# Two pages' first layers interwoven, the decoding of the dense weights reordered, and 512-column products in the dense layer

## The chip, the cores and the metric

The kernel runs on one core of one Trainium2 chip. The metric is the device time of one execution in microseconds (us). Engines are named as in the profile: PE (TensorE, matmuls; PEld its weight loads), DVE (VectorE), ACT (ScalarE), POOL (GpSimd) and SP (SyncE, which here only issues transfers). Each engine works off its own instructions in the order of the program; waits between engines are on semaphores.

## The reference

```python
def reference(x, expert_emb, tau, w1, w2, w_in, w_out):
    X = np.fft.fft(np.fft.fft(x, axis=1), axis=2).real        # x: 8 x 3072 x 256
    x = X.reshape(24576, 256)
    # routing: cosine of each token with 8 expert vectors, one expert a token
    xn = x / (norm(x) + 1e-6); en = expert_emb / (norm(expert_emb) + 1e-6)
    logits = xn @ en.T / tau
    e = argmax(logits, axis=1); gate_w = softmax(logits)[arange, e]
    y = gate_w[:, None] * (maximum(x @ w1[e], 0) @ w2[e])     # 256 -> 1024 -> 256
    # dense layer for every token
    h = y @ w_in                                              # 256 -> 2048
    return maximum(0.01 * h, h) @ w_out                       # 2048 -> 256
```

All is float32. `w_in` and `w_out` come as 64-bit floats, which the kernel takes apart itself.

## The kernel before

**Batches.** The two FFTs of a batch of 3072 tokens (`batch`) are matmuls with tables of sines and cosines between folds on DVE: folds (label `f`, L399 to L315), the stage along the sequence (`s_stage`, label `s`), then column tiles (`unit`, label `d`: two matmuls of L446, ACT's `cs`, DVE's `xo`), which also give the routing logits. `route` (label `r`) finds each token's expert and place, `pages` the list of pages; then POOL scatters 24 lists into the DRAM tables (label `sc`, L599). Batch 0 runs ahead of everything; batches 1 to 7 run as generators, a few labels in each step of the main loop, with a budget per step: each label has a weight (`WEIGHT`), and what is left of `WORK` is spread evenly over the steps up to a limit. `MARGIN` and `NEAR` set that limit for batch 1.

**Pages.** Tokens of one expert are gathered in pages of 256. There are 89 full pages, 21 half slots for what is left over, and seven pages made of those: 96 that go through the dense layer. `load_page` (SP) reads a page's entries of the three tables, `fetch_page` merges them on DVE (`merge`, L874 to L880) and gathers the rows with POOL; `transpose` turns them on PE into `xt`. `wload` (SP) loads a quarter of an expert's weights into one of two `raw` buffers, `wsplit` splits it in two parts (ACT L919 the high one, DVE L920 the rest).

**Steps.** A product of two float32 numbers is made of three fp32r products: high x high, high x low, low x high (`PASS`). The main loop goes over a list `steps` of (kind, page, s). Kind 1 is the expert layer in four steps: `m1_a` makes 256 columns of h (L941, twelve matmuls), `m1_b` adds them to `y` (L959). Kind 2 is the dense layer in eight steps: `m2_a` (L1014) and `m2_b`, which adds to `o` (L1045). Kind 3 is a half slot: its first layer (L973) has 512 columns to a matmul. Each step issues its a-part, then the b-part of a step `LAG` = 3 earlier (2 in the first steps). ACT and DVE make `hh` from `h` in between. After a page's eighth `m2_b`, ACT scales the two halves of `o` (L1051) and POOL scatters them to the output. PSUM has eight banks: two `a`, three `h`, two `o`, one `y`.

**Decoding.** `decodes` takes `w_in` and `w_out` apart in 16 pieces; `decode` is one piece of seven DVE instructions (L740 to L754) and three ACT copies. Before, two pieces run side by side, instruction by instruction, and the next two load when both are done. Six pieces (`NDEC`) run within batch 0, at a pace of steps per label (`RAMP`); the others within the first steps of the pages, seven instructions in a step (`DREST`).

Of the kernel before, what the change touches and what calls it, by code (L numbers as in the profile page):

```python
# [6 lines left out]
F32 = mybir.dt.float32  # L7
# [51 lines left out]
class K:  # L59
# [314 lines left out]
    def batch(self, b):  # L374
# [51 lines left out]
        if b:  # L426
            yield "f"
            yield "f"
        z = [mp.tile([128, 1537], F32, tag=f"z{j}", name="z") for j in range(2)]
# [87 lines left out]
    def route(self, b, rt, lr, n2, sli, tb, i0, i1):  # L517
# [54 lines left out]
        if b:  # L572
            yield "r"
            yield "r"
        pr = self.pa()[:, 0:E * (nt + 1)].rearrange("p (i e) -> p i e", e=E)
# [154 lines left out]
    def decode(self, raw, hi, lo, temps):  # L730
# [7 lines left out]
        nc.scalar.activation(b, lw.bitcast(U32), AF.Copy, scale=2.0 ** -52)  # L738
# [11 lines left out]
        V.tensor_tensor(b, b, t.bitcast(F32), op=ALU.mult)  # L750
# [5 lines left out]
    def decodes(self):  # L756
# [12 lines left out]
        raws = {}  # L769
        self.ndec = 0  # L770

        def load(i, tile):
            raws[i] = tile
            nc.sync.dma_start(out=tile if pieces[i][1] is None else tile.rearrange("p (c d) -> p c d", c=2), in_=pieces[i][0])

        def unit(i, temps):
            return self.decode(raws.pop(i).rearrange("p (f w) -> p f w", w=2), *pieces[i][2:], temps)


        def buf(i):  # L780
            if i < 2:
                return self.xp.tile([128, 1024], F32, tag="raw", name="rawd", bufs=2).bitcast(I32)
            return self.ip.tile([128, 1024], I32, tag="rawd", name="rawd", bufs=2)

        def temps():
            return [self.ip.tile([128, 512], F32, tag=f"dec{i}", name="dec", bufs=2) for i in range(3)]

        for i in range(4):
            load(i, buf(i))
        yield  # L790
        for i in range(0, NDEC, 2):
            pair = [unit(i + k, temps) for k in range(2)]
            while pair:
                for g in list(pair):
                    if next(g, "end") == "end":
                        pair.remove(g)
                        self.ndec += 1
                    else:
                        yield
            for k in range(2):  # L800
                if i + 4 + k < NDEC:
                    load(i + 4 + k, buf(2))
            yield
# [528 lines left out]
```

## Time and profile before

| | |
|---|---|
| Median of three runs | 3684.71 us (3683.41 to 3685.48) |
| The profiled execution | 3683.92 us, span 3682.2 us |
| PE busy | 3532.7 us, 96% of the span, 29441 matmuls |
| PE weight loads busy | 3501.5 us, 95% |
| DVE busy | 2334.4 us, 63% |
| ACT busy | 1933.6 us, 53% |
| POOL busy | 672.2 us, 18% |
| Mean granted clock of PE | 0.982 of 2.4 GHz |

Busy shares are means over the whole span. PE is busy 0.4 of the first two of 40 slices (92 us each) and 0.8 or more of every later one, so the first 200 us are read apart from the rest.

### The profile page before, as it was taken

Reading aid. Unit: us, or ns where it says so; the run is one execution under the profiler, and the core shown is the slowest. Engines: PE = TensorE matmul, PEld = TensorE weight load, DVE = VectorE, ACT = ScalarE, POOL = GpSimd, SP = SyncE. Lnnn points to the kernel's source line nnn. Section 1 sums busy time; section 2 is a strip of 40 time slices with the busy share of each in tenths; the row PEclk is TensorE's granted clock in tenths of the full one; section 3 lists DMA queues with packets and bytes.
Section 4 is the critical chain, followed back from the end, with each engine's and each line's share of the span. In section 5 each row is a group of like instructions: output and inputs, shape, how many; then the busy total and the mean of one; then the engine's idle time right before and its main releaser. Section 6 shows DMA issues by size and latency. Waiting matters only on the chain.

```text
span 3682.2 us, 74898 instructions
## 1 busy us (share of the span) xinstructions
PE 3532.7 (96%) x29441; PEld 3501.5 (95%) x29441; DVE 2334.4 (63%) x4595; ACT 1933.6 (53%) x3491; POOL 672.2 (18%) x620
## 2 busy tenths in 40 slices
PE   4498999999999999999999999999999999999998
PEld 3388999999999999999999999999999999999998
DVE  7575666567565666657565675657666566666644
ACT  3345446455554546445464455544565456666543
POOL 3113111311013110321114111231114111111100
PEclk8699999999999999999999999999999999999999
DMA  4332413233232322233132322223232245555300
GB/s 141 126 109 71 145 60 115 66 113 96 73 107 71 134 82 99 74 102 104 60 120 73 120 76 86 94 81 124 76 105 76 72 132 155 153 152 155 104 25 16
DMA packets 266165, 362.58 MB, mean 98 GB/s; under 512 B 75984, under 2 KB 216659, under 8 KB 265620
## 3 DMA queue, kind: packets, MB, share of 16 engines
q1 hardware_dynamic: 238896, 303.66, 25.9%
q0 software_dynamic: 25184, 52.35, 4.5%
q8 instruction: 230, 3.77, 0.4%
q10 hardware_dynamic: 1732, 1.79, 0.1%
q14 instruction: 123, 1.01, 0.1%
HBM read 304.64 MB, written 63.41 MB: 100 GB/s over the span
## 4 chain that ended last, share of the span: by engine, by line
PE 86%; issue 3%; DMA 1%; DVE 0%; ACT 0%; POOLq 0%; SPq 0%; POOL 0%; ACTq 0%
PE o L1045 27%; PE h L1014 26%; PE h L941 13%; PE y L959 13%; PE y L986 2%; PE h L973 2%; PE a L926 1%; PE a L446 1%; DMA out<-ob,tab 1%; PE a L1030 0%; PE a L339 0%; PE a L340 0%; PE a L337 0%; DMA raw<-w 0%; PE a L334 0%
## 5 line engine op out<-in xcount | busy, mean ns | idle before, releaser
L1045 PE MATMUL o<-wo,hh 128*128 128x256 f32 x9216 | 1233.9, 283 | 9.4 <-DVE hh L1034 9.4
L1014 PE MATMUL h<-yt,wi 128*128 128x256 f32 x9216 | 1217.1, 281 | 14.4 <-ACT yt L963 14.2
L1045 PEld LDWEIGHTS o<-wo,hh 128*128 128x128 f32 x9216 | 1148.5, 189 | 13.4 <-DVE hh L1034 10.0
L1014 PEld LDWEIGHTS h<-yt,wi 128*128 128x128 f32 x9216 | 1137.9, 189 | 14.8 <-ACT yt L963 14.4
L1016 ACT ACTIVATE g<-h 128x512 f32<-128x512 f32 x768 | 457.6, 596 | 788.0 <-PE h L1014 786.7
L1017 DVE TENSOR_TENSOR g<-g,h 128x512 f32<-128x512 f32 x768 | 525.9, 685 | 459.9 <-ACT g L1016 456.3
L1052 POOL DMA_INDIRECT out<-ob,tab x192 | 214.8, 1119 | 2298.7 <-ACT ob L1051 1932.4
L920 DVE TENSOR_TENSOR w<-raw,w 128x1024 fp32r<-128x1024 f32 x440 | 536.9, 1224 | 151.7 <-ACT w L919 148.6
L944 DVE SCALAR_TENSOR_TENSOR hh<-h,hh 128x512 fp32r<-128x512 f32 x356 | 246.2, 691 | 548.8 <-ACT hh L943 548.7
L941 PE MATMUL h<-xt,w 128*128 128x256 f32 x4272 | 563.4, 281 | 17.1 <-ACT xt L928 14.8
L959 PE MATMUL y<-hh,w 128*128 128x256 f32 x4272 | 567.6, 282 | 8.4 <-ACT w L919 7.1
L941 PEld LDWEIGHTS h<-xt,w 128*128 128x128 f32 x4272 | 530.4, 190 | 18.8 <-ACT xt L928 15.7
L959 PEld LDWEIGHTS y<-hh,w 128*128 128x128 f32 x4272 | 529.8, 189 | 9.9 <-ACT w L919 7.5
L1034 DVE TENSOR_TENSOR hh<-g,hh 128x512 fp32r<-128x512 f32 x768 | 525.9, 685 | 1.4 <-ACT hh L1033 1.3
L919 ACT ACTIVATE w<-raw 128x1024 fp32r<-128x1024 f32 x440 | 462.1, 1055 | 89.1 <-DMA raw<-w 86.7
L1033 ACT ACTIVATE hh<-g 128x512 fp32r<-128x512 f32 x768 | 479.3, 624 | 26.2 <-DVE g L1017 25.7
L943 ACT ACTIVATE hh<-h 128x512 fp32r<-128x512 f32 x356 | 212.8, 598 | 518.5 <-PE h L941 518.2
L897 POOL DMA_INDIRECT xr<-xd,tab x199 | 240.1, 1207 | 539.8 <-issue 314.1
L599 POOL DMA_INDIRECT table<-tb,sli x192 | 210.1, 1094 | 161.1 <-DVE tb L593 54.1
L1051 ACT ACTIVATE ob<-o,tf 128x256 f32<-128x256 f32 x192 | 80.6, 471 | 76.7 <-PE o L1045 76.5
L926 PE MATMUL a<-ident,xr 128*128 128x128 f32 x426 | 66.6, 274 | 38.8 <-DMA xr<-xd,tab 38.8
L928 ACT ACTIVATE xt<-a 128x512 fp32r<-128x512 f32 (+1 forms) x110 | 61.1, 555 | 75.3 <-PE a L926 74.1
(291 smaller groups left out, 1766.6 us busy)
## 6 DMA issues: line engine op xcount, KB each, us to landing
raw<-w SPq DMA_DIRECT2D x440, 512.0 KB
x<-xl SPq DMA_DIRECT2D x32, 768.0 KB
xd<-xo SPq DMA_DIRECT2D x96, 256.0 KB
table<-bigd SPq DMA_DIRECT2D x21, 384.0 KB
t<-table SPq DMA_DIRECT2D x267, 4.0 KB
xr<-xd,tab POOLq DMA_INDIRECT x199, 4.7
table<-tb,sli POOLq DMA_INDIRECT x192, 3.0
rawz<-w_out SPq DMA_DIRECT2D x6, 512.0 KB
```

The lines of the kernel that those rows point to most:

```text
L897: nc.gpsimd.indirect_dma_start(out=self.xr[seq[u] % NX][:, h], out_offset=None, in_=self.xd[0:rows, :], in_offset=bass.IndirectOffsetOnAxi ...
L919: nc.scalar.activation(hi, r, AF.Copy)
L920: V.tensor_tensor(lo, r, hi.bitcast(F32), op=ALU.subtract)
L941: nc.tensor.matmul(p[:, f], self.w1[:, wa, dc, fc * 128:(fc + 1) * 128], xt[:, xa, dc], start=(k == 0), stop=(k == 5))
L944: V.scalar_tensor_tensor(h[:, 1], p, 0.0, h[:, 0].bitcast(F32), op0=ALU.max, op1=ALU.subtract)
L959: nc.tensor.matmul(y[:, x], self.w2[:, wa, fc, xs_], h[:, ha, f], **st)
L1014: nc.tensor.matmul(p[:, f], self.wi[:, wa, dc, fc * 128:(fc + 1) * 128], yt[:, xa, dc], start=(k == 0), stop=(k == 5))
L1016: nc.scalar.activation(g, p, AF.Copy, scale=0.01)
L1017: V.tensor_tensor(g, g, p, op=ALU.max)
L1033: nc.scalar.activation(h[:, 0], g, AF.Copy)
L1034: V.tensor_tensor(h[:, 1], g, h[:, 0].bitcast(F32), op=ALU.subtract)
L1045: nc.tensor.matmul(o[:, th], h[:, xa, f, th * 128:(th + 1) * 128], self.wo[:, wa, fc], start=(fc == 0 and th == 0 and k == 0), stop=(fc == ...
```

## The change

**The order of the first steps.** The expert layer of page 1 is interwoven with the dense layer of page 0: page 0's dense steps 0, 1, 2 and 3 stand between and behind the last three expert steps of page 1. Page 1 is transposed one step earlier, into a buffer of its own (`yt`'s, since `xt` has one). The b-parts of the last expert steps of pages 0 and 1 follow one step behind their a-parts, and the lag is 2 for the first 20 steps. Weight splits are tied to the places of the page's own steps.

**Decoding.** Two pieces run staggered by four instructions, and when one ends the next begins (`rolling`). Three buffers before, four later (two z tiles and two x tiles) are loaded ahead. The ACT copy of the low word is gone; a DVE instruction of the same count reads the word itself. In the s stage of batch 0 two instructions go with each label instead of one; ten more decoding steps stand between the page list and the split of page 0's w1, 14 between that and the merge of page 0, eight ahead of the merge of page 1 (`FIRST`); afterwards three in a step instead of seven. SP loads page 0's w2 ahead of its table entries.

**Batch 1** has weights of its own (`WEIGHT1`, `WORK1`), must be done two steps earlier (`MARGIN`), and ends its share of a step at two places by a label `next`.

**The wide product.** From page 2 on, `m2_b` multiplies the high part of `hh` by the high and low parts of `wo` in one matmul of 512 columns, into a bank per half page, and the low part by the high one in a matmul of 256. The two sums lie side by side in the bank: ACT scales the second, DVE multiplies the first and adds.

```diff
-FIRST = 0, 0
+FIRST = 10, 14, 8
+SHORT = 20
+SKEW = 4
+RLOAD = 1
-MARGIN = 6, 1
+MARGIN = 6, 3
 WEIGHT = {'f': 8, 's': 4, 'd': 4, 'r': 4, 'sc': 4}
 WORK = 522
+WEIGHT1 = {'f': 8, 's': 8, 'd': 16, 'r': 5, 'sc': 8}
+WORK1 = 858
-NDEC, DREST, RA, RAMP = 6, 7, (4, 4, 4, 0, 0, 0), {'i': 5, 's': (1, 1), 'd': (0, 1), 'r': (1, 1), 'sc': (1, 1)}
+NDEC, DREST, RA, RAMP = 6, 3, (4, 4, 4, 0, 0, 0), {'i': 5, 's': (2, 1), 'd': (0, 1), 'r': (1, 1), 'sc': (1, 1)}
...
-        nc.scalar.activation(b, lw.bitcast(U32), AF.Copy, scale=2.0 ** -52)
...
-        V.tensor_tensor(b, b, t.bitcast(F32), op=ALU.mult)
+        V.scalar_tensor_tensor(b, lw.bitcast(U32), 2.0 ** -52, t.bitcast(F32), op0=ALU.mult, op1=ALU.mult)
...
+        def unit(i):
+            yield from self.decode(raws.pop(i).rearrange("p (f w) -> p f w", w=2), *pieces[i][2:], lambda: temps(i))
+            self.ndec += 1
+            k = i + (3 if i < NDEC else 4)
+            if (2 <= i and k < NDEC) or (i >= NDEC and k < last):
+                load(k)
+
+        def rolling(i, end):
+
+            run = [unit(i)]
+            i += 1
+            n = 0
+            while run:
+                for g in list(run):
                     if next(g, "end") == "end":
+                        run.remove(g)
+                        if i < end:
+                            run.append(unit(i))
+                            i += 1
+                            next(run[-1])
+                    yield
+                    n += 1
+                    if n == SKEW and i < end:
+                        run.append(unit(i))
+                        i += 1
...
-        steps = [(1, u, s) for u in range(PRE - 1) for s in range(4)]
-
-        steps += [(1, PRE - 1, s) for s in range(4)]
-        for q in range(4):
+        steps = [(1, 0, s) for s in range(4)]
+
+
+        steps += [(1, 1, 0), (1, 1, 1), (2, 0, 0), (1, 1, 2), (2, 0, 1), (1, 1, 3), (2, 0, 2), (2, 0, 3)]
+        steps += [(2, 1, s) for s in range(4)]
+        for q in range(2, 4):
...
+            wide = u >= PRE
             if s == 0:
-                ops[u] = self.ps("o", [128, 2, D], 2)
+                ops[u] = [self.ps("o", [128, 2, D], 2) for _ in range(2 if wide else 1)]
...
+                    nc.tensor.matmul(o[th], h[:, 0, f, tk], self.wo[:, :, fc], start=(fc == 0), stop=False, skip_group_check=True)
+                    nc.tensor.matmul(o[th][:, 0], h[:, 1, f, tk], self.wo[:, 0, fc], start=False, stop=(fc == 15), skip_group_check=True)
...
-                    nc.scalar.activation(ot, o[:, th], AF.Copy, scale=tf[:, 4 * th + 2:4 * th + 3])
+                    w = tf[:, 4 * th + 2:4 * th + 3]
+                    if not wide:
+                        nc.scalar.activation(ot, o[0][:, th], AF.Copy, scale=w)
+                    else:
+                        nc.scalar.activation(ot, o[th][:, 1], AF.Copy, scale=w)
+                        V.scalar_tensor_tensor(ot, o[th][:, 0], w, ot, op0=ALU.mult, op1=ALU.add)
...
+                if lab == "r" and n == RLOAD:
+                    for i in range(NDEC, NDEC + 3):
+                        self.load_piece(i)
...
+            while more:
+                more = next(dec) != "rest"
+            self.load_piece(NDEC + 3)
+            for _ in range(FIRST[0]):
+                next(dec)
             wsplit(0, 0)
             wsplit(0, 1)
-            load_page(0)
             wload(0, 2)
             wload(0, 3)
-            while more:
-                more = next(dec) != "rest"
+            load_page(0)
+            for _ in range(FIRST[1]):
+                next(dec)
             fetch_page(0)
             load_page(1)
...
+        def lag(n):
+
+            return 1 if steps[n] in ((1, 0, 3), (1, 1, 3)) else LAG if n > SHORT else 2
```

Three places in the order of the engines. Lines of the changed kernel have other numbers; there L748 to L762 are the seven instructions of `decode`, L879 to L885 the merge, L931 a transpose, L947 and L965 the two parts of the expert layer, L1020 and L1056 those of the dense layer, L1059 and L1060 the wide and the narrow product of it, L453 a column tile.

DVE between the last pieces decoded within batch 0 and the first page, before:

```order
L750 TENSOR_TENSOR dec<-dec 128x512 x2
L752 TENSOR_TENSOR dec<-dec,wi 128x512 x2
L754 TENSOR_TENSOR wi<-dec 128x512 x2
L920 TENSOR_TENSOR w_76<-raw,w_76 128x1024 x2
L874 TENSOR_TENSOR tf<-t_920 128x8
L875 TENSOR_TENSOR tf<-tf,t_920 128x8
L880 CAST tab<-tf 128x4
L874 TENSOR_TENSOR tf<-t_948 128x8
L875 TENSOR_TENSOR tf<-tf,t_948 128x8
L880 CAST tab<-tf 128x4
L929 TENSOR_TENSOR xt<-a,xt 128x512
```

And now, from within the decoding that stands ahead of page 0's merge to that ahead of page 1's:

```order
L758 SCALAR_TENSOR_TENSOR dec<-rawx,dec 128x512
L748 TENSOR_SCALAR dec<-dec 128x512
L760 TENSOR_TENSOR dec<-dec,wi 128x512
L750 TENSOR_SCALAR dec<-dec 128x512
L879 TENSOR_TENSOR tf<-t_943 128x8
L880 TENSOR_TENSOR tf<-tf,t_943 128x8
L885 CAST tab<-tf 128x4
L762 TENSOR_TENSOR wi<-dec 128x512
L752 SCALAR_TENSOR_TENSOR dec<-rawx,dec 128x512
L754 TENSOR_SCALAR dec<-dec 128x512
L748 TENSOR_SCALAR dec<-dec 128x512
L758 SCALAR_TENSOR_TENSOR dec<-rawx,dec 128x512
```

Before, all the seven-instruction pieces of batch 0's time are done ahead of the split of w1 (L920), and nothing stands between that and the merges (L874). Now 22 instructions of decoding stand between the page list and the first merge (the last four of them shown), and eight between the two merges (the first five shown).

PE in the first two pages, from the first m1_b of page 0 on, before:

```order
L959 MATMUL y<-hh,w_77 128x256 x12
L941 MATMUL h<-xt,w_76 128x256 x12
L959 MATMUL y<-hh,w_77 128x256 x12
L926 MATMUL a<-ident,xr_125 128x128 x4
L941 MATMUL h<-xt,w_76 128x256 x12
L959 MATMUL y<-hh,w_77 128x256 x12
L941 MATMUL h<-xt,w_76 128x256 x12
L959 MATMUL y<-hh,w_77 128x256 x12
L941 MATMUL h<-xt,w_76 128x256 x12
L959 MATMUL y<-hh,w_77 128x256 x12
L941 MATMUL h<-xt,w_76 128x256 x12
L959 MATMUL y<-hh,w_77 128x256 x12
```

And now:

```order
L965 MATMUL y<-hh,w_77 128x256 x12
L931 MATMUL a<-ident,xr_125 128x128 x4
L947 MATMUL h<-xt,w_76 128x256 x12
L965 MATMUL y<-hh,w_77 128x256 x12
L947 MATMUL h<-yt,w_76 128x256 x12
L965 MATMUL y<-hh,w_77 128x256 x24
L947 MATMUL h<-yt,w_76 128x256 x12
L1020 MATMUL h<-yt,wi 128x256 x12
L965 MATMUL y<-hh,w_77 128x256 x12
L947 MATMUL h<-yt,w_76 128x256 x12
L965 MATMUL y<-hh,w_77 128x256 x12
L1020 MATMUL h<-yt,wi 128x256 x12
```

The transpose of page 1 (xr_125) stands ahead of page 0's last expert step instead of behind it; and page 0's dense step (h<-yt,wi) stands between page 1's expert steps, where there were those alone.

PE while batch 1's column tiles (L446, a<-gt,z) are made, before:

```order
L959 MATMUL y<-hh,w_77 128x256 x12
L1014 MATMUL h<-yt,wi 128x256 x12
L446 MATMUL a<-gt,z 128x137 x6
L959 MATMUL y<-hh,w_77 128x256 x12
L1014 MATMUL h<-yt,wi 128x256 x12
L446 MATMUL a<-gt,z 128x137 x6
L959 MATMUL y<-hh,w_77 128x256 x12
L1014 MATMUL h<-yt,wi 128x256 x12
L446 MATMUL a<-gt,z 128x137 x6
L959 MATMUL y<-hh,w_77 128x256 x12
L1014 MATMUL h<-yt,wi 128x256 x12
L446 MATMUL a<-gt,z 128x137 x8
```

And now, at the end of that stretch, with the first wide block of page 2:

```order
L453 MATMUL a<-gt,z 128x137 x2
L965 MATMUL y<-hh,w_77 128x256 x12
L1020 MATMUL h<-yt,wi 128x256 x12
L453 MATMUL a<-gt,z 128x137 x4
L1059 MATMUL o<-wo,hh 128x512
L1060 MATMUL o<-wo,hh 128x256
L1059 MATMUL o<-wo,hh 128x512
L1060 MATMUL o<-wo,hh 128x256
L1059 MATMUL o<-wo,hh 128x512
L1060 MATMUL o<-wo,hh 128x256
L1059 MATMUL o<-wo,hh 128x512
L1060 MATMUL o<-wo,hh 128x256
```

Three or four tiles (two matmuls each) stood in a step, now there are one or two. A block of twelve matmuls of L1045 is now four pairs of L1059 and L1060.

## Rows read from the trace of the kernel before

**Rows 1.** Busy time by stage: edges, length, each engine's busy us (instructions), PEclk, DMA.
```profile
0.00:113.18 113.18, 36.91 (x198) 34.26 (x199) 77.64 (x322) 36.89 (x103) 39.21 (x63) 0.76 0.41 137
113.18:227.28 114.10, 74.97 (x505) 71.65 (x505) 83.76 (x166) 50.19 (x80) 4.91 (x4) 0.77 0.39 134
227.28:380.43 153.15, 133.70 (x1058) 130.14 (x1056) 89.49 (x232) 75.73 (x166) 42.84 (x39) 0.94 0.28 89
380.43:3682.20 3301.77, 3287.16 (x27686) 3265.45 (x27684) 2083.49 (x3878) 1770.78 (x3143) 585.22 (x515) 1.00 0.31 96
```

**Rows 2.** PE's waits, 113 to 400 us: waiting line, releaser, total us, times, longest.
```profile
PE a L926 <- DMA xr<-xd,tab: 38.8, 4, 36.8
PE h L941 <- ACT xt L928: 14.8, 3, 12.0
PE h L1014 <- ACT yt L963: 14.2, 1, 14.2
PE o L1045 <- DVE hh L1034: 9.4, 3, 7.3
PE y L959 <- ACT w L919: 7.1, 2, 5.4
PE a L446 <- DVE xo L481: 5.9, 3, 2.4
PE a L576 <- DVE ohb L570: 2.8, 1, 2.8
```

**Rows 3.** Timeline of PE in the steady part: start, us, instructions.
```profile
1501.95 1.56 PE L1014 MATMUL h<-yt,wi 128*128 128x256 f32 x12
1503.34 1.59 PE L1045 MATMUL o<-wo,hh 128*128 128x256 f32 x12
1504.77 0.60 PE L926 MATMUL a<-ident,xr 128*128 128x128 f32 x4
```

**Rows 4.** Timeline of PE, first layer of a rest page.
```profile
2986.16 1.56 PE L973 MATMUL h<-w,xt 128*128 128x512 f32 x6
2987.56 1.57 PE L1045 MATMUL o<-wo,hh 128*128 128x256 f32 x12
```

**Rows 5.** Groups by line and shape, whole kernel: busy us, mean ns; idle, releaser.
```profile
L1051 ACT ACTIVATE ob<-o,tf 128x256 f32<-128x256 f32 x192 | 80.6, 471 | 76.7 <-PE o L1045 76.5
...
L366 DVE SCALAR_TENSOR_TENSOR z<-a,ptmp 128x256 f32<-128x256 f32 x29 | 12.1, 419 | 3.1 <-PE a L340 1.4 <-PE a L337 1.1 <-ACT ptmp L361 0.6
```

**Rows 6.** Timeline of DVE, two pieces of weights decoded side by side.
```profile
151.09 0.75 DVE L742 TENSOR_SCALAR dec<-dec 128x512 int32<-128x512 int32 x2
151.76 1.29 DVE L744 SCALAR_TENSOR_TENSOR dec<-rawz,dec 128x512 int32<-128x512 int32 x2
152.97 0.76 DVE L746 TENSOR_SCALAR dec<-dec 128x512 int32<-128x512 int32 x2
```

**Rows 7.** Timeline of POOL, first and last of 24 scatters of batch 0.
```profile
66.07 1.05 POOL L599 DMA_INDIRECT table<-tb,sli  x1 [54.07 <-DVE tb L593]
...
102.93 0.98 POOL L599 DMA_INDIRECT table<-tb,sli  x1 [0.30 <-issue]
```

**Rows 8.** Timeline of DVE ahead of the first page; idle time before in brackets.
```profile
95.39 2.52 DVE L920 TENSOR_TENSOR w<-raw,w 128x1024 fp32r<-128x1024 f32 x2 [0.21 <-ACT w L919]
...
106.55 0.17 DVE L874 TENSOR_TENSOR tf<-t 128x8 f32<-128x8 f32 x1 [8.64 <-DMA t<-table]
...
113.52 0.17 DVE L874 TENSOR_TENSOR tf<-t 128x8 f32<-128x8 f32 x1 [5.42 <-DMA t<-table]
```

**Rows 9.** Groups by line and shape, whole kernel, a fold of the FFT.
```profile
L299 DVE TENSOR_TENSOR f<-w 128x192 f32<-128x192 f32 x64 | 19.8, 350 | 0.0
```

**Rows 10.** Timeline of POOL and DVE, scatters of batch 1 and the merge behind them.
```profile
326.37 1.77 POOL L599 DMA_INDIRECT table<-tb,sli  x1 [0.31 <-DVE rg L661]
...
360.01 0.98 POOL L599 DMA_INDIRECT table<-tb,sli  x1 [0.30 <-issue]
...
364.31 0.17 DVE L874 TENSOR_TENSOR tf<-t 128x8 f32<-128x8 f32 x1 [11.89 <-DMA t<-table]
```

More of the change, by code (lines that the diff above doesn't have):

```diff
@@ L768, in decodes @@
                 pieces.append((src, 2, *dst))
-        raws = {}
+        raws, last = {}, len(pieces)
         self.ndec = 0
[L772 to L780, printed above, removed]
-            if i < 2:
-                return self.xp.tile([128, 1024], F32, tag="raw", name="rawd", bufs=2).bitcast(I32)
-            return self.ip.tile([128, 1024], I32, tag="rawd", name="rawd", bufs=2)
@@ L785, in temps @@
[L785 to L789, printed above, removed]
-        yield
[L791 to L803, printed above, removed]
@@ L804, in decodes, with load @@
-        yield "rest"
-        def zbuf(i):
-            return mp.tile([128, 1537], F32, tag=f"z{i % 2}", name="rawz").bitcast(I32)[:, 0:1024]
-        def gtemps(j):
-            tags = ("s3k", 3), (f"f{j}0", 1), (f"f{j}1", 1)
-            return [mp.tile([128, 768], F32, tag=t, name="dec", bufs=n)[:, 0:512] for t, n in tags]
-        for k in range(2):
-            load(NDEC + k, zbuf(k))
-        yield
-        for i in range(NDEC, len(pieces), 2):
-            pair = [unit(i + k, lambda k=k: gtemps(k)) for k in range(2)]
-            while pair:
-                for g in list(pair):
-                    if next(g, "end") == "end":
-                        pair.remove(g)
-                        self.ndec += 1
-                    else:
-                        yield
-            for k in range(2):
-                if i + 2 + k < len(pieces):
-                    load(i + 2 + k, zbuf(k))
-            yield
+        def load(i):
+            if i < 2:
+                t = self.xp.tile([128, 1024], F32, tag="raw", name="rawd", bufs=2).bitcast(I32)
+            elif i < NDEC:
+                t = self.ip.tile([128, 1024], I32, tag="rawd", name="rawd", bufs=3)
+            elif (i - NDEC) % 4 < 2:
+                t = mp.tile([128, 1537], F32, tag=f"z{(i - NDEC) % 4}", name="rawz").bitcast(I32)[:, 0:1024]
+            else:
+                t = mp.tile([128, 1536], F32, tag="x", name="rawx", bufs=2).bitcast(I32)[:, 0:1024]
+            raws[i] = t
+            nc.sync.dma_start(out=t if pieces[i][1] is None else t.rearrange("p (c d) -> p c d", c=2), in_=pieces[i][0])
@@ new lines, in temps @@
+        def temps(i):
+            if i < NDEC:
+                return [self.ip.tile([128, 512], F32, tag=f"dec{k}", name="dec", bufs=2) for k in range(3)]
+            tags = ("s3k", 3), (f"f{i % 2}0", 1), (f"f{i % 2}1", 1)
+            return [mp.tile([128, 768], F32, tag=t, name="dec", bufs=n)[:, 0:512] for t, n in tags]
+        def unit(i):
[4 more added lines that the diff above has]
+                load(k)
@@ L832, in main @@
+        self.load_piece = load
+        for i in range(5):
+            load(i)
+        yield
+        yield from rolling(0, NDEC)
+        yield "rest"
+        yield from rolling(NDEC, last)
     def main(self):
@@ L1062, in main @@
         ls = (0, 0)
+        pos = {s: i for i, s in enumerate(steps)}
         firsts = [(i, u) for i, (m, u, s) in enumerate(steps) if m != 2 and s == 0]
@@ L1129, in main @@
         self.wide = False
-        for _ in range(FIRST[0]):
+        for _ in range(FIRST[2]):
             next(dec)
         fetch_page(1)
-        for _ in range(FIRST[1]):
-            next(dec)
         transpose(0)
@@ L1185, in main @@
                 split_g()
-            while done < len(steps) and i - done >= (LAG if done > 4 * PRE else 2):
+            while done < len(steps) and i - done >= lag(done):
                 m, u, s = steps[done]
```

35 lines of the change are left out of this document (24 added, 11 removed).

## The prediction

> **What bounds the kernel now.** I read the busy time by stage first, then TensorE's list of waits, then its timeline at three places, then the queues of the engines that it waited for. Four stretches matter [rows 1]; their edges are first matmuls, of page 0 (113.18), page 2 (227.28) and page 5 (380.43). From 380 us to the end PE is busy 3287.16 of 3301.77 us at full granted clock: there only fewer or cheaper matmuls help. Ahead of 113 us PE has almost nothing to do; the FFT of batch 0, its routing and the decoding of the dense weights run on DVE, and POOL scatters the page lists. From 113 to 227 us PE is busy 74.97 of 114.10 us, at a mean granted clock of 0.77 of 2.4 GHz, while DVE is busy 83.76: neither is full, they wait for each other. From 227 to 380 us PE still loses 19.45 us, and its clock is 0.94. The waits say on whom [rows 2]: ACT's xt, yt and w (14.8, 14.2 and 7.1 us), mostly while decoding goes on; DVE's hh (9.4, of which 7.3 in one piece) and xo (5.9) while batch 1 is transformed. So there are two places for a gain: some 55 us of loss between 113 and 380 us, and the price of a block of matmuls after it.
>
> **The wide product.** For 94 of 96 pages the block that adds to o issues four pairs of 128x512 and 128x256 in place of twelve 128x256: 3008 pairs, the same 3072 columns a block, eight weight loads instead of twelve. A block of L1045 takes 1.43 us (1503.34 to 1504.77) and one of L1014 1.39 (1501.95 to 1503.34) [rows 3]. The only rows with 512 columns are those of L973: six of them, 3072 columns again, in 1.40 us (2986.16 to 2987.56) [rows 4], 0.233 us each, nearly twice the 0.119 of a 256 in L1045. So the time goes with columns, and hardly with instructions or weight loads. Two thirds of the new block at L973's pace (0.93) and a third at L1045's (0.475) make 1.405 against 1.425 (the pace of L1045 lies between 1.42 and 1.43 in its rows): 0.018 us, with 94 x 8 = 752 blocks 13 us. The bounds: at best the whole block at 1.395, 23 us; at worst the excess of L1045 over L1014, which both have the same columns, comes from reading wo as the moving operand and grows by as much again with a read of two runs: 0.035 us a block, 26 us lost. L973 also moves weights and is nearest; I take 13.
> The Trainium skill ("TensorE: Matmul & The Clock Gate", Back-to-back issue gap) gives about 131 ns for a matmul of 512 columns in a stream with weight loads. By that a pair would take 131 + 119 = 250 ns instead of three times 119, and 3008 pairs would give 322 us. L973's 233 ns says no.
>
> **The evacuation of o.** Each wide page now holds both o buffers, and after its last product come ACT's scaled copy (0.47 us) and, new, a DVE multiply-add per half; the nearest DVE row is L366, 0.42 us on 256 columns read from PSUM [rows 5]. That is 188 x 0.42 = 79 us more on DVE, which after 380 us is busy 2083 of 3302 us [rows 1]: hidden. The next page's first o block must wait for it: last product, 0.47, 0.42, some 0.2 us between engines, about 1.1 us for the first half and 0.47 later for the second. For most pages four steps of another page's first layer stand between, over 10 us of PE work. Where page follows page without them (page 4, and the seven of the tail) the cover is one L1014 block, 1.39 us, and the second half is wanted about 0.35 us after the first: 0 to 0.5 us, eight times, at most 4 us; I take 1, and about 0.4 us at the very end, where the last output goes through DVE first. Together 13 becomes 12.
>
> **The front.** Ahead of the first xo DVE's queue now holds 22 decode instructions instead of 10. One piece is seven, three at 0.335 us and four at 0.605 by the distances of starts [rows 6], 0.49 on average; twelve more are 5.9 us. Some fall in holes of a DVE that is busy 77.64 of 113.18 us, so I put xo and all behind it 3.5 us later (0 to 6). POOL's 24 scatters are one chain from 66.07 to 103.91 us [rows 7], the page table comes with its end, and so moves by the same 3.5. The decoding that was put between the page list and the first page fills what was idle: DVE stood 8.64 and 5.42 us before the two merges of page lists [rows 8]; now 22 of 30 further decode instructions stand ahead of the first merge and 8 ahead of the second, 14.7 us in 14.1 us of holes. Since xt of page 0 is queued behind the last eight, some with a raw piece that SP loads only after the page table, I add 1 us. The first product comes 4.5 us later (0 to 9). The w2 loads now stand ahead of the page table on SP, and wait for DVE's splits of w1; those start at 95.39 [rows 8], 8.5 us ahead of the scatters' end, with twelve decode instructions between page list and splits, now eight. So this costs nothing unless DVE is later by more than that; then the page table is late by the rest.
>
> **Pages 0 and 1.** The second stretch then has 40 decode instructions instead of 70: DVE's 83.8 us fall by 14.7. By the same step it has done some 18 more fold instructions of batch 1 (order of DVE; 0.31 us each, L299 as the dearer of two kinds [rows 9]), 5.5 us: 74.6 us busy. Its idle time was 30.3 us. What made it idle is decoding in pairs: both pieces load only after the pair before is done, ACT stands in order before that load, and behind it the w, xt and yt that PE waits for [rows 2]. Now four raw buffers are loaded ahead, two pieces run four instructions apart, and page 0's dense steps stand between page 1's steps, so that PE has work while w2 of page 1 is split. I take 13 us of idle time, between 5 (only splits of weights behind their loads are left) and 30.3 (nothing changes). The stretch takes 87.6 us instead of 114.1, 26.5 less; with the later start 22, between 0 and 34. DVE is then the limit, so PE's nominal work doesn't set the sum.
>
> **Batch 1.** Its transform starts three steps later and its work is spread by new weights, one or two column tiles in a step where there were three or four (order, below). With two banks a third tile in a step makes PE wait for xo: those 5.9 us go. The page list is done two steps earlier, a step being one h and one o block, 2.8 us [rows 3]: the 24 scatters from 326.37 to 360.99 us, whose end DVE waited for 11.89 us in a merge, with hh behind it [rows 10], end 5.6 us earlier against PE, and PE's 7.3 us fall to 1.7. L576's 2.8 us stay, as do some 4 us for pages 5 and 6, whose rows and weights come late either way (2.0 of L926's 38.8 beside its first wait of 36.8, and about 2 of xt's). The clock, 0.94 over 153 us, is worth 9 us; with half of the stalls gone I take 3 back. Together 14.5 us, between 4 (the list is no earlier) and 20.
>
> **The sum** against the profiled execution, 3683.92 us with a span of 3682.2, 0.8 below the median of the three runs: 12 + 22 + 14.5 = 48.5 us, 3635 us.
>
> **Rivals.** (1) The ramp gives little: DVE stays idle as long as before, since the raw pieces and expert weights share one DMA queue and each split still waits for its load, and what is won is lost in the denser folds. For it: the DVE work falls by only 9 us in the stretch. Against: the idle time stands behind pairs that are gone. Ramp 0 to 16 us, wide 12: 3656 to 3672. (2) The ramp gives its gain, the wide block costs what the old one cost: then 3647 (3636 to 3659). (3) The other side: pages wait for their o buffers. Place: the first o block of a page, behind ACT's and DVE's queues, which at the page's end hold g and hh of the step as well. It decides from 0.6 us a page: 94 pages x 0.6 us are more than the 36.5 us of the ramp and the wide product's 13 together. At the full evacuation, 2 x 0.47 + 0.42 us a page, 128 us lost less 49: 3763. For it: both buffers belong to one page now. The Trainium skill ("Perfetto Trace Analysis", Matmuls) wants independent groups to rotate through banks, so that one's evacuation overlaps the next one's matmuls, which speaks against this edit; no row here shows the wait. Against: over 10 us of cover for 86 pages. (4) The edits do nothing that lasts, gain and loss cancel: 3677 to 3692. (5) Weight loads set PE's pace after all: PEld is busy 3265 of 3302 us [rows 1], and a third fewer loads in o at 0.119 us each give 358 us, 3326. Against: L973 has half the loads of L1014 for the same columns and takes the same time.
>
> **How the numbers follow.** The likeliest 0.62, with its own range 3612 to 3652; (1) 0.17; (2) 0.10; (3) 0.04; (4) 0.05; (5) 0.02. Two runs of this kernel tell 0.2% apart, 7.4 us. Faster by more: the likeliest, (1), (2) and (5), 0.91; within it (4), 0.05; slower (3), 0.04. From 3610 to 3669 lie nearly all of the likeliest, most of (1) and (2): a bit over 0.8.
>
> **What would show it.** Pairs of L1059 and L1060 at 0.35 us, blocks near 1.40; first product of page 0 near 118 us; page 2's first matmul near 205; page 5's near 344; xo no longer in PE's waits, the merge's wait near 6 us. It is wrong if a block stays at 1.42 or more, if PE waits for ob or o's multiply-add between pages, or if w, xt and yt hold PE between 118 and 205 us as long as before.

## The result, and the profile after

The changed kernel takes 3644.45 us (median of four runs, 3642.00 to 3647.56), the kernel before 3684.06 in the runs beside it: 39.6 us less, a ratio of 0.9896 (95% interval 0.9880 to 0.9911). The forecast was 3635 us, 48.5 less. The profiled execution took 3645.73 us, its span is 3644.0.

The busy time by stage, with the edges of [rows 1] (first matmuls of page 0, page 2 and page 5) and the same columns:

```profile
0.00:123.50 123.50, 38.26 (x199) 35.05 (x199) 93.73 (x355) 38.09 (x106) 37.82 (x63) 0.72 0.48 156
123.50:210.78 87.28, 71.87 (x517) 68.06 (x518) 72.79 (x146) 38.32 (x61) 4.47 (x4) 0.90 0.37 120
210.78:348.92 138.14, 128.15 (x962) 121.25 (x960) 87.44 (x223) 75.11 (x165) 42.88 (x40) 0.96 0.34 108
348.92:3644.00 3295.08, 3279.50 (x24762) 3128.10 (x24760) 2159.95 (x4062) 1767.94 (x3143) 585.99 (x514) 1.00 0.32 96
```

In us:

| Stretch | before | predicted | after |
|---|---|---|---|
| to page 0's first matmul | 113.18 | 117.7 | 123.50 |
| pages 0 and 1 | 114.10 | 87.6 | 87.28 |
| to page 5's first product | 153.15 | 138.65 | 138.14 |
| the rest | 3301.77 | 3289.8 | 3295.08 |
| span | 3682.2 | 3633.7 | 3644.0 |

Two stretches came out within 0.6 us of the forecast; the front lost 5.8 us more than forecast, the rest gave 5.3 less.

PE's waits from 113 to 400 us, as in [rows 2]:

```profile
PE a L931 <- DMA xr<-xd,tab: 43.0, 1, 43.0
PE o L1056 <- DVE hh L1040: 8.2, 9, 1.4
PE o L1059 <- DVE ob L1070: 6.9, 1, 6.9
PE h L947 <- ACT xt L933: 3.6, 2, 2.9
PE h L947 <- ACT w L924: 2.1, 1, 2.1
...
PE h L1020 <- DVE yt L970: 1.1, 1, 1.1
...
PE a L453 <- DVE xo L488: 0.3, 1, 0.3
```

The waits for xt and yt fell from 14.8 and 14.2 us to 3.6 and 1.1, that for xo from 5.9 to 0.3. New are short waits for hh while DVE is busy 83% of the stretch of pages 0 and 1, and one wait of 6.9 us for the o bank. That one is the merge's wait of [rows 10] in another place. Timeline of POOL, then DVE, then PE:

```profile
326.36 0.98 POOL L608 DMA_INDIRECT table<-tb,sli  x1 [0.30 <-issue]
```

```profile
330.04 0.17 DVE L879 TENSOR_TENSOR tf<-t 128x8 f32<-128x8 f32 x1 [7.41 <-DMA t<-table]
...
332.64 0.87 DVE L1070 SCALAR_TENSOR_TENSOR ob<-o,tf,ob 128x256 f32<-128x256 f32 x2
```

```profile
333.17 0.79 PE L1059 MATMUL o<-wo,hh 128*128 128x512 f32 x1 [6.88 <-DVE ob L1070]
```

The last scatter of batch 1 starts at 326.36 (360.01 before), DVE stands in the merge until the table arrives, and behind the merge now stand the multiply-adds for which the next page's first o block waits.

In the front the scatters of batch 0 start 4.0 us later than in [rows 7] and end 10.0 us later. Timeline of POOL, and of DVE behind it:

```profile
70.08 1.05 POOL L608 DMA_INDIRECT table<-tb,sli  x1 [58.05 <-DVE tb L602]
...
79.89 0.98 POOL L608 DMA_INDIRECT table<-tb,sli  x1 [2.65 <-DMA table<-tb,sli]
...
101.79 1.05 POOL L608 DMA_INDIRECT table<-tb,sli  x1 [3.36 <-DMA table<-tb,sli]
...
112.96 0.98 POOL L608 DMA_INDIRECT table<-tb,sli  x1 [0.30 <-issue]
```

```profile
117.46 0.17 DVE L879 TENSOR_TENSOR tf<-t 128x8 f32<-128x8 f32 x1 [6.95 <-DMA t<-table]
```

From first to last scatter it is 42.9 us instead of 36.9: POOL waits for transfers of earlier scatters.

The steady part, PE's timeline at the place of [rows 3]:

```profile
1499.38 1.57 PE L1020 MATMUL h<-yt,wi 128*128 128x256 f32 x12
1500.79 0.39 PE L1059 MATMUL o<-wo,hh 128*128 128x512 f32 x1
1501.03 0.28 PE L1060 MATMUL o<-wo,hh 128*128 128x256 f32 x1
1501.14 0.39 PE L1059 MATMUL o<-wo,hh 128*128 128x512 f32 x1
...
1502.18 1.58 PE L1020 MATMUL h<-yt,wi 128*128 128x256 f32 x12
```

A pair takes 0.35 us and this o block 1.39; but the h block ahead of it takes 1.41, where it took 1.39 before. (At the median behind page 5's first product, an o block fell from 1.420 to 1.403 and a dense h block rose from 1.400 to 1.411.) Added up from the starts of all blocks behind page 5's first product: the o blocks fell from 1046.7 to 1033.1 us, by 13.6; the h blocks of the dense layer rose by 3.6, those of the expert layer by 2.9, and the rest by 0.4. That leaves 6.7.

### The profile page after: what moved, and what is told of

It is laid out like the page before. It is cut to its first block, busy times and chain, and to the rows that moved or that the text cites. A ratio compares the mean times of both kernels' runs of the same rounds, so it can differ in the third digit from the quotient of the medians.

```text
span 3644.0 us, 69226 instructions
## 1 busy us (share of the span) xinstructions
PE 3517.8 (97%) x26433; PEld 3352.5 (92%) x26433; DVE 2413.9 (66%) x4783; ACT 1919.5 (53%) x3475; POOL 671.2 (18%) x620
## 5 line engine op out<-in xcount | busy, mean ns | idle before, releaser
L1020 PE MATMUL h<-yt,wi 128*128 128x256 f32 x9216 | 1216.6, 281 | 1.1 <-DVE yt L970 1.1
L1020 PEld LDWEIGHTS h<-yt,wi 128*128 128x128 f32 x9216 | 1135.8, 189 | 14.5 <-DVE yt L970 1.3
L1059 PE MATMUL o<-wo,hh 128*128 128x512 f32 x3008 | 1104.1, 400 | 6.9 <-DVE ob L1070 6.9
L1060 PE MATMUL o<-wo,hh 128*128 128x256 f32 x3008 | 844.5, 281 | 0.0
L1059 PEld LDWEIGHTS o<-wo,hh 128*128 128x128 f32 x3008 | 566.1, 188 | 109.6 <-DVE ob L1070 7.1
L1060 PEld LDWEIGHTS o<-wo,hh 128*128 128x128 f32 x3008 | 568.7, 189 | 1.6
L965 PE MATMUL y<-hh,w 128*128 128x256 f32 x4272 | 566.1, 282 | 1.9 <-DVE w L925 1.3
L947 PE MATMUL h<-xt,w 128*128 128x256 f32 x4224 | 557.4, 282 | 4.6 <-ACT xt L933 3.6
L947 PEld LDWEIGHTS h<-xt,w 128*128 128x128 f32 x4224 | 524.5, 190 | 19.6 <-ACT xt L933 4.3
L965 PEld LDWEIGHTS y<-hh,w 128*128 128x128 f32 x4272 | 528.7, 189 | 3.0 <-DVE w L925 1.5
L1039 ACT ACTIVATE hh<-g 128x512 fp32r<-128x512 f32 x768 | 479.0, 624 | 13.1 <-DVE g L1023 12.5
L931 PE MATMUL a<-ident,xr 128*128 128x128 f32 x426 | 66.0, 274 | 43.0 <-DMA xr<-xd,tab 43.0
```

What stands on the lines that cost most here:

```text
L947: nc.tensor.matmul(p[:, f], self.w1[:, wa, dc, fc * 128:(fc + 1) * 128], xt[:, xa, dc], start=(k == 0), stop=(k == 5))
L965: nc.tensor.matmul(y[:, x], self.w2[:, wa, fc, xs_], h[:, ha, f], **st)
L1020: nc.tensor.matmul(p[:, f], self.wi[:, wa, dc, fc * 128:(fc + 1) * 128], yt[:, xa, dc], start=(k == 0), stop=(k == 5))
L1039: nc.scalar.activation(h[:, 0], g, AF.Copy)
L1059: nc.tensor.matmul(o[th], h[:, 0, f, tk], self.wo[:, :, fc], start=(fc == 0), stop=False, skip_group_check=True)
L1060: nc.tensor.matmul(o[th][:, 0], h[:, 1, f, tk], self.wo[:, 0, fc], start=False, stop=(fc == 15), skip_group_check=True)
```

## The experiments

Twelve kernels ran, on four chips, each beside the kernel before on its own chip. On three of them that one took 3702 to 3708 us, on the fourth 3682.37; so ratios and traces are compared, and times only within a chip. "Page 5" below is page 5's first product, "page 2" that of page 2, "the list" the start of batch 1's last scatter; stretches and waits are those of one profiled execution of each kernel.

### The wide product: e1, e2, e8

e1 is the changed kernel without it:

```diff
-            wide = u >= PRE
+            wide = False
```

> The changed kernel with narrow products (twelve of 256 columns) for all pages; all else stays. Read from page 5's first product to the end, 3295.1 us in the changed kernel. Theory A, as predicted: a wide block saves its own 0.018 us and nothing else changes, so that stretch becomes 12 to 13 us longer (3307 to 3308). Theory B, from the trace after: the wide blocks save 13.6 us, but the block behind each (next h) grows from 1.394-1.400 to 1.410-1.414 us and gives 6.9 us back, so the stretch becomes 6.7 us longer (3301 to 3302) and h blocks go back to 1.394-1.400. Theory C: the wide product gives nothing, the stretch stays within 2 us. The whole: the o buffers' wait of 6.9 us near 326 us and the lower clock behind it (some 2.5 us) go or shrink in each theory, because ACT alone empties o: A 3647 to 3657, B 3642 to 3651, C 3635 to 3644.

e2 puts the new `m2_b` whole into the kernel before.

> The kernel before with the wide product alone. From page 5's first product to the end the kernel before takes 3301.8 us. Theory A: 3289 to 3290. Theory B: 3295, with h blocks at 1.410-1.414 us behind wide ones. Theory C: 3301. Ahead of that, the merge that waits 11.89 us for batch 1's page list now has a multiply-add of o behind it, so PE may wait there longer than its 7.3 us for hh, by up to 4 us. The whole, beside 3684: A 3671 to 3676, B 3677 to 3681, C 3684 to 3688.

e8 is the changed kernel with a block's wide products first and its narrow ones behind them:

```diff
-                    nc.tensor.matmul(o[th][:, 0], h[:, 1, f, tk], self.wo[:, 0, fc], start=False, stop=(fc == 15), skip_group_check=True)
+            if wide:
+                for f in range(2):
+                    for th in range(2):
+                        fc = 2 * s + f
+                        nc.tensor.matmul(o[th][:, 0], h[:, 1, f, th * 128:(th + 1) * 128], self.wo[:, 0, fc], start=False, stop=(fc == 15), skip_group_check=True)
```

> The changed kernel with the four wide products of a block first and its four narrow ones behind them, instead of pairs. If the growth of the next h block comes from the alternation of widths (or from the wide instruction close before it), it goes or the wide block changes: h blocks at 1.394-1.400 us, 3637 to 3640. If it comes with any block that has wide products, h blocks stay at 1.410-1.414 us: 3642 to 3647. If the widths cost more apart (six loads of weights close together behind narrow ones), the block is above 1.403 us: over 3647.

On one chip, before 3707.61 us: e1 3679.60 (ratio 0.9920, 0.9907 to 0.9932), e2 3711.45 (1.0004, 0.9990 to 1.0017), e8 3693.34 (0.9950, 0.9933 to 0.9966). The blocks of e1, then of e8, in PE's timeline:

```profile
1533.12 1.56 PE L947 MATMUL h<-xt,w 128*128 128x256 f32 x12
1534.52 1.58 PE L1056 MATMUL o<-wo,hh 128*128 128x256 f32 x12
1535.94 1.56 PE L947 MATMUL h<-xt,w 128*128 128x256 f32 x12
1537.34 1.56 PE L965 MATMUL y<-hh,w 128*128 128x256 f32 x12
```

```profile
1533.10 1.57 PE L947 MATMUL h<-xt,w 128*128 128x256 f32 x12
1534.51 1.09 PE L1059 MATMUL o<-wo,hh 128*128 128x512 f32 x4
1535.44 0.63 PE L1064 MATMUL o<-wo,hh 128*128 128x256 f32 x4
1535.91 1.57 PE L947 MATMUL h<-xt,w 128*128 128x256 f32 x12
1537.32 1.57 PE L965 MATMUL y<-hh,w 128*128 128x256 f32 x12
```

With narrow products the o block is back at 1.42 and the h block at 1.40; that is theory B's coupling. Grouped, the o block falls to 1.40, but now h and y blocks stand at 1.41. What this is worth from page 5 on is read from the mean of each kind of block, without the few over 1.7 us, which hold waits:

| | o | h, dense | h, expert | y | all of them |
|---|---|---|---|---|---|
| blocks | 731 | 728 | 336 | 336 | |
| narrow: before, e1 | 1.440 | 1.415 | 1.404 | 1.417 | 3030.3, 3030.6 us |
| pairs: the changed kernel | 1.421 | 1.420 | 1.410 | 1.416 | 3021.9 us |
| groups: e8 | 1.423 | 1.421 | 1.414 | 1.425 | 3028.3 us |

The other ten kernels with pairs, on all chips, have 3021.7 to 3023.0 us. So pairs gain some 8 us: o blocks win some 13.6 and the h blocks behind them give back some 6. Groups gain 2, because y gives back too. Theories A (12 to 13 us) and C (nothing) are out for the pace of the blocks.

The stretch itself, where PE does not starve (that is, has no waits without a named releaser; see the end): 3301.8 us before; 3295.1, 3293.9, 3297.0 and 3293.6 in the changed kernel, e9, e10 and e4. Where it starves, e1 takes 3328.9 (page 5 at 351.32, span 3680.2) and c1, which loses about as much to such waits there (13.0 us, e1 11.9), 3322.0; e3 takes 3318.1, e8 3345.2. So the wide product is worth some 5 to 8 us of the stretch. Whole times on the starving chips don't show it: e2 is where theory C has it (1.0004), and e1's ratio is that of c1 (0.9920 and 0.9918). What hides it in e2 stays open; its page 5 comes at 385.40, and no trace of the kernel before was taken on that chip.

### The merge of page 5: e3, e9

In e3 it stands three steps later:

```diff
-                at(min(k + GAP if n < 10 else max(k + GAP, i - 8), i - 3), fetch_page, u)
+                at(min(k + GAP + (3 if u == 5 else 0) if n < 10 else max(k + GAP, i - 8), i - 3), fetch_page, u)
```

e9 has 1 in place of 3.

> The changed kernel with the merge of page 5's list (first of batch 1) three steps later in DVE's order. Theory: DVE waits 7.4 us in it for the table, with the multiply-adds of o of page 3 behind it, and that makes PE's 6.9 us at the first o block of page 4, and the lower clock behind it. Then both go: 3635 to 3639, page 5's first product some 6 to 9 us ahead of 348.9 us. Rival: page 5's rows come that much later and PE waits for them instead, 3642 to 3646.

> The changed kernel with the merge of page 5's list one step later, so that it stands behind the multiply-adds of o of page 3 on DVE instead of ahead of them. Theory: PE's wait of 6.9 us for ob, and the lower clock behind it, go; the table still comes when it came, so page 5's rows do too, and PE waits for these or for hh 0 to 4 us instead: from the last h block of page 4 ahead of the wait to page 5's first product 16 to 20 us instead of 24.2. Rival: the wait moves to hh in full, 22 to 25 us, as with the merge three steps later (21.3 us, there for the rows).

e3: 3691.71 us (0.9951, 0.9934 to 0.9968), on the chip of e1. e9: 3647.12 (0.9907, 0.9892 to 0.9922) beside 3682.37. PE in e9:

```profile
334.72 0.38 PE L1060 MATMUL o<-wo,hh 128*128 128x256 f32 x1 [2.39 <-DVE hh L1040]
...
341.02 0.48 PE L931 MATMUL a<-ident,xr 128*128 128x128 f32 x1 [4.49 <-DMA xr<-xd,tab]
```

The wait for the o bank is gone and comes back as 2.39 us for hh and 4.96 for page 5's rows (4.49 and a second piece of 0.47); page 5 is at 349.69, where it was at 348.92. In e3 PE also waits for the rows, 4.2 us, and page 5 comes at 361.22, some 10 us behind e1 (351.32) and e8 (348.58) on the same chip. The rivals held: one step later neither wins nor loses, because the table comes only when the list is done; three steps later puts page 5 off.

### What made the first 350 us shorter: c1, e5, e6, e7

c1 is the changed kernel again, for a measure on the same chip.

> The changed kernel again, beside the kernel before on the same chip, as the measure for the other runs sent with it: on this work's first chip 0.9896 of before; on the chip of the runs e1, e2, e3 and e8 the kernel before took 3707 us instead of 3684, PE idle some 20 us with no releaser while POOL scatters the page lists. If that hits the changed kernel as often as the kernel before, the ratio stays at 0.988 to 0.991; if it hits wide products more, the ratio is 0.992 to 0.997.

e5 has batch 1's settings of before:

```diff
-MARGIN = 6, 3
+MARGIN = 6, 1
...
-            gens.append([beg, lim, self.batch(b), WORK1 if b == 1 else WORK + (LASTWORK if b == NB - 1 else 0), 0, WEIGHT1 if b == 1 else WEIGHT])
+            gens.append([beg, lim, self.batch(b), WORK + (LASTWORK if b == NB - 1 else 0), 0, WEIGHT])
...
                         if lab == "next":
-                            break
+                            continue
```

> The changed kernel with batch 1's weights, work, margin and pauses as before. Theory, as predicted: these give 14.5 us between page 2's first matmul and page 5's first product (138.1 us in the changed kernel): now 149 to 154 us, xo back among PE's waits with some 6 us, the wait in the merge near 12 us; 12 to 16 us slower than the changed kernel. Rival: most of those 15 us came from the decoding that is over sooner and from the clock, 141 to 145 us, 3 to 7 us slower.

e6 decodes in pairs, in place of the staggered loop of `rolling` (the loads go into the two z tiles):

```diff
+            for a in range(i, end, 2):
+                run = [unit(a), unit(a + 1)]
+                while run:
+                    for g in list(run):
+                        if next(g, "end") == "end":
+                            run.remove(g)
+                        yield
+                if i >= NDEC:
+                    for k in (a + 2, a + 3):
+                        if k < end:
+                            load(k)
+                            yield
```

> The changed kernel with decoding in pairs: two pieces side by side, instruction by instruction, the next two loaded when both are done, into two buffers; the order of the pages' steps stays as changed. Theory, as predicted: DVE's idle time in the first two pages came from the pairs, so the stretch from page 0's first product to page 2's first matmul (85.4 us from 125.4 to 210.8 in the changed kernel) grows by 10 to 17 us, and the whole by as much. Rival: the interweaving gives the gain, the stretch grows by at most 4 us.

e7 has the order of steps of before:

```diff
-        steps = [(1, 0, s) for s in range(4)]
-        steps += [(1, 1, 0), (1, 1, 1), (2, 0, 0), (1, 1, 2), (2, 0, 1), (1, 1, 3), (2, 0, 2), (2, 0, 3)]
-        steps += [(2, 1, s) for s in range(4)]
-        for q in range(2, 4):
+        steps = [(1, u, s) for u in range(PRE) for s in range(4)]
+        for q in range(4):
```

> The changed kernel with the order of steps of before (all of page 1's expert layer, then the dense layers of pages 0 and 1 in turns of two steps); decoding and all else as changed. Theory, as predicted: PE waits again while w2 of page 1 is split, with nothing of page 0 to do, but DVE sets the pace of the stretch, so it grows by 2 to 6 us. Rival: without the interweaving the stretch grows by 10 us or more, since PE then stands at every split and DVE behind PE.

| | median us | ratio (interval) | page 2 | the list | page 5 |
|---|---|---|---|---|---|
| c1 | 3673.73 | 0.9918 (0.9896 to 0.9940) | 208.24 | 324.38 | 350.12 |
| e5 | 3683.42 | 0.9951 (0.9934 to 0.9968) | 206.47 | 339.17 | 362.02 |
| e6 | 3689.81 | 0.9969 (0.9957 to 0.9981) | 204.75 | 343.86 | 366.00 |
| e7 | 3668.63 | 0.9909 (0.9894 to 0.9924) | 211.93 | 326.79 | 352.76 |

e5: the stretch from page 2 to page 5 grows from 141.9 to 155.6 us, 13.7 where 14.5 were forecast for these edits; the whole loses 9.7, where 12 to 16 were expected. xo is back among PE's waits in e5:

```profile
PE a L453 <- DVE xo L488: 5.8, 3, 2.5
```

Of the other parts DVE's wait in the merge did not go back to 12 us (6.64). e6: the whole loses 16.1 us, as the theory had it, but not in its place: from page 0's first product to page 2 it is even shorter (75.4 us, c1 82.9). The loss is that the decoding ends at 197.5 us instead of 180.7, so batch 1 starts later and its list ends 19.5 us later. One cause is a row of DVE in e6:

```profile
119.42 0.43 DVE L748 TENSOR_SCALAR dec<-dec 128x512 f32<-128x512 f32 x1 [13.37 <-ACT dec L746]
```

DVE stands 13.37 us because the next raw pieces load only when both are done, and then behind the page table on SP. e7: the stretch of pages 0 and 1, from page 0's first product, grows by 3.6 us (86.5), page 5 comes 2.6 us later. The rival's 10 us are out; that the theory's 2 to 6 are right is not shown, for the five other traces of kernels that are the same up to page 2 (the changed kernel, e1, e3, e8, e9) lie between 83.2 and 85.8. The runs of c1 spread over 26 us, so its median tells nothing of this.

### The front: e4, e10, e11

e4 loads the four raw pieces behind both page lists, and so can decode none of them ahead of the first page; e10 has the first two lines of this diff alone:

```diff
-FIRST = 10, 14, 8
+FIRST = 0, 0, 0
...
-                if lab == "r" and n == RLOAD:
-                    for i in range(NDEC, NDEC + 3):
-                        self.load_piece(i)
...
-            self.load_piece(NDEC + 3)
...
             load_page(1)
+            for i in range(NDEC, NDEC + 4):
+                self.load_piece(i)
```

> The changed kernel with the four raw pieces for the pages' decoding loaded behind both page tables, and so with none of the 32 decoding instructions ahead of the first transposes. The 24 scatters of batch 0 take 42.9 us from first to last in the changed kernel, 36.9 in the kernel before. Theory A: the raw pieces' transfers beside the scatters hold POOL; then the chain is back at 36 to 38 us, first product of page 0 at 116 to 120 us instead of 125. Theory B: it is DVE's dense decoding; then the chain also falls here, but the run e10 falls with it. Theory C: neither, 41 us or more. The whole loses: 32 instructions, some 16 us of DVE work, move behind the first product, where DVE is nearly full: page 5's first product within 5 us of the changed kernel's, earlier or later.

> The changed kernel with its raw pieces loaded at the same place, but none of the 32 decoding instructions ahead of the first transposes. Theory A (transfers hold POOL): the chain of scatters stays at 41 to 43 us, page 0's first product at 123 to 126 us. Theory B (DVE's decoding holds POOL): the chain falls to 36 to 39 us, first product at 117 to 121 us.

First and last scatter of batch 0, and the last of batch 1, in e10, then the last of batch 0 in e4 (its first is at 71.21):

```profile
71.84 1.05 POOL L608 DMA_INDIRECT table<-tb,sli  x1 [59.69 <-DVE tb L602]
...
114.64 0.98 POOL L608 DMA_INDIRECT table<-tb,sli  x1 [0.30 <-issue]
...
345.27 0.98 POOL L608 DMA_INDIRECT table<-tb,sli  x1 [0.50 <-DMA table<-tb,sli]
```

```profile
110.95 0.98 POOL L608 DMA_INDIRECT table<-tb,sli  x1 [0.30 <-issue]
```

42.8 us in e10, 39.7 in e4: the 32 instructions of DVE's decoding do not hold POOL, so B is out, though A's 36 to 38 us are not reached. The raw pieces' transfers are 3.1 of the 6 us, by one trace of each (the other kernels that load them in the same place as the changed one lie between 41.9 and 43.9). The rest stays open; in e4 POOL still waits 1.30 and 0.50 us just behind the w2 loads of 102 us, which stood behind the chain before, and 2.64 us ahead of them. e4's first product came no earlier all the same (126.27): the raw pieces then run beside page 0's rows, and PE waits for those.

The times say more: 3664.08 (e4, 0.9954, 0.9940 to 0.9967) and 3663.41 us (e10, 0.9949, 0.9936 to 0.9963), while e9 on the same chip, whose page 5 comes as in the changed kernel, takes 3647.12. So the 32 instructions ahead of the first transposes are worth 16.3 us, their own length (32 x 0.49 = 15.7), and they cost nothing: e10's first product comes at 125.85 us, the changed kernel's at 125.36. The loss is not seen at page 2 (209.19) but at the list (345.27) and page 5 (366.42). In e4 page 5 comes at 368.69, far from the 5 us around the changed kernel's that were expected.

e11 fills DVE's hole ahead of the first merge:

```diff
-            load_page(0)
             for _ in range(FIRST[1]):
                 next(dec)
+            load_page(0)
+            for _ in range(12):
+                next(dec)
             fetch_page(0)
```

> The changed kernel with twelve more instructions of decoding ahead of the first merge (34 instead of 22), and SP's load of page 0's list behind the loads of the next two raw pieces, so that these don't wait for the scatters. DVE stands 6.95 us idle ahead of that merge in the changed kernel. Theory: each decoding instruction done in that hole is worth its own length later, as the 32 of the run e10 were (16 us): the hole falls to about 1 us, page 5's first product comes 5 to 6 us earlier, 0.9880 of before instead of 0.9896. Rival: the two raw pieces move beside the last scatters and the page's rows; the first product comes 3 us later or more, and page 5's stays within 2 us.

3666.75 us, 0.9914 (0.9893 to 0.9934): not faster. The hole is filled and the decoding ends at 171 us instead of 183.5, but the list comes at 332.73 and page 5 at 354.31, 5.4 us later than in the changed kernel (4.2 later than in c1). DVE in e11, ahead of batch 1's first fold:

```profile
118.61 0.17 DVE L879 TENSOR_TENSOR tf<-t 128x8 f32<-128x8 f32 x1 [1.17 <-DMA t<-table]
...
179.25 0.96 DVE L404 TENSOR_TENSOR u<-x 128x768 f32<-128x768 f32 x1 [6.49 <-DMA x<-xl]
```

Of what was won 6.49 us go in a wait for batch 1's input, which SP issues at 172.62, behind page 1's weights. The fold still starts 5.4 us earlier than in the changed kernel (184.65). But PE's waits for w and yt in pages 0 and 1 grew (4.0 and 6.3 us in one piece each), and page 2 comes at 225.24 instead of 210.78. Which of these delays the list is not shown.

## Why the prediction was right, step by step

**The whole.** The forecast said 3635 us, within 3610 to 3669; it is 3644.45. The two places of the gain are the forecast ones: page 5 comes 31.5 us earlier, and the stretch behind it is 6.7 us shorter. Rivals (1) and (4), by which the first 380 us give little, are out with the 31.5 us, and (2), by which the wide block costs what the old one did, with the 8 us that its blocks gain. But the account of what happens ahead of page 5 was only in part right, and two terms agree better than their reasons do.

**What sets page 5.** The prediction added up stretches of PE. The runs show one chain under them: DVE's decoding, DVE's folds and routing of batch 1, POOL's scatters, the merge, the rows. Page 5's first product comes 20 to 24 us behind the start of the list's last scatter before (360.01, 380.43), after (326.36, 348.92) and in eight of the twelve runs; 25 to 28 in c1, e1 and e7, where PE starves near it, and 34 in e3, which put the merge off. The list came 33.65 us earlier, page 5 31.5. The terms of the front, pages 0 and 1 and batch 1, together 36.5 us forecast and 31.5 measured, all end in that chain. They are not separate shares of it: undone one at a time, the edits of e5, e6 and e7 (against c1) and of e10 (against e9) put page 5 back by 11.9, 15.9, 2.6 and 16.7 us, 47 together. (The "some 55 us of loss" that the prediction starts from are 58.6 by its own rows, 39.13 and 19.45; nothing in the sum hangs on it.)

**Pages 0 and 1.** 87.28 us against 87.6, DVE busy 72.79 against 74.6. That the number fits is luck as far as its reason goes: "what made it idle is decoding in pairs" is not what made this stretch long. With pairs (e6) it takes 79.0 us from page 0's first matmul to page 2, less than c1's 85.9; with the old order of steps (e7) 89.4, without the 32 instructions ahead (e10) 86.2, where it was 114.1 before. No edit undone alone brings it back, and what shortened it is not shown. The gain of the new decoding is shown in the whole (e6, 16.1 us), but it pays at the list.

**Batch 1.** 138.14 against 138.65. That these edits bring it is shown by e5 (13.7 of 14.5 us), and of the parts xo (5.9 to 0.3, back at 5.8 in e5). The merge's part failed: PE's wait of 7.3 us, forecast to fall to 1.7, is 6.88 at the o bank. That the sum fits all the same is luck.

**The front.** This step was mis-sized: 10.3 us later instead of 4.5, outside its own 0 to 9. DVE's part was right (the first scatter is 4.0 us later, 3.5 forecast). "POOL's 24 scatters are one chain" that "moves by the same 3.5" was wrong: it also grew by 6.0, about half of it by the raw pieces beside it (e4 against e10). On the end it cost less than it looks, since decoding filled the wait.

**The wide product.** Mis-sized too: 12 us forecast, 6.7 measured. The block's own gain was right, 13.6 against 13. The step that failed is that the neighbours would stay: h blocks behind wide ones grew, by 0.011 us at the median, and took half of it back (e1 and e8 show the coupling). An estimate from the figure of the Trainium skill ("TensorE: Matmul & The Clock Gate", Back-to-back issue gap), about 131 ns for 512 columns, made it 322 us; the trace disagrees, with 0.230 to 0.235 us from a 512-column product to the next start (medians by place in the block). Rival (5), weight loads as the pace, is out: PEld's busy time fell from 3265 to 3128 us behind page 5, and the stretch by 6.7.

**The evacuation.** No page change behind page 5 has a wait for o in PE's list; the cover held. Rival (3)'s place, and with it one of the prediction's own signs of being wrong, showed once, with 6.88 us at page 4, where 0 to 0.5 were forecast, because DVE stood in a merge; that e9 takes it away and gains nothing shows that it cost no more than the list did. The Trainium skill ("Perfetto Trace Analysis", Matmuls) wants independent groups to rotate through banks, so that one's evacuation overlaps the next one's matmuls; in the changed kernel's trace giving that up cost a wait only here, where the engine that empties the bank was itself waiting.

## What to carry to other kernels

Before adding up gains by stretches of the busiest engine, look for the one result that the next stage can't start without (here a page list) and follow the chain that makes it: work taken off that chain can pay at its end even if the stretch in which it was taken off gets no shorter (e6, e10). Gains found by undoing one edit at a time need not add up to the gain of all of them. Filling an engine's idle time on such a chain is not a gain by itself: the twelve instructions of e11 ended the decoding 12.5 us earlier and brought the list 6.4 us later than in the changed kernel. And when a block is made cheaper, measure its neighbours too, and by means: the medians of these blocks hide the gain.

## What was not expected of the hardware

A block's pace depends on its neighbours. With the same 3072 columns and a granted clock of 1.00, the h block behind pairs takes 1.411 us at the median instead of 1.400, and behind groups the y block, too, 1.413 instead of 1.400, so that nearly half (pairs) or most (groups) of what the o blocks win is lost. Why stays open.

On three of four chips PE stood idle with nothing that the profile names as its releaser, at the times when POOL scatters page lists. The runs of the first chip and e4, e9 and e10 have no such wait; PE's waits in c1 have these:

```profile
PE h L1020 <- issue: 12.7, 19, 1.5
...
PE o L1059 <- issue: 4.5, 8, 0.8
...
PE o L1060 <- issue: 3.8, 5, 1.6
```

Of these 21 us 13.0 lie behind page 5's first product, all of them beside the scatters of a list. They are half of the 26.9 us that separate c1's stretch from page 5 on (3322.0 us) from the 3295.1 us of the same kernel; more goes at the lower clock around them (a mean granted clock of 0.91 from 680 to 700 us, where the changed kernel has 1.00 on the first chip). What PE waits for was not tried.
